# Scores of the late units in 64-column products, a remainder formed by TensorE, and a new order of work

## The chip, the cores and the metric

The kernel runs on one core of a Trainium2 chip. Its time is the device time of one execution in microseconds; several executions are timed and the median is given. The engines named below are TensorE (PE in the rows, PEld its weight loads), VectorE (DVE), ScalarE (ACT), GpSimd (POOL) and SyncE (SP), which issues DMAs.

## What is computed

A gated linear attention with complex gates gives a matrix x of 3072 rows and 384 columns, and a two-layer network with a Gelu is applied to it. Cut to what matters (B = 4, H = 8, S = 768, D = 48, 2048 hidden columns):

```python
scale = np.minimum(mag, 0.999) / (mag + 1e-06)     # mag = |a|
a_re_n, a_im_n = a_re * scale, a_im * scale
for t in range(S):
    ar, ai = a_re_n[:, :, t, :, None], a_im_n[:, :, t, :, None]
    new_re = ar * S_re - ai * S_im
    new_im = ar * S_im + ai * S_re
    S_re, S_im = new_re + k_t[..., None] * v_t[..., None, :], new_im
    y[:, :, t] = einsum('bhd,bhde->bhe', q[:, :, t], S_re)
x = y.transpose(0, 2, 1, 3).reshape(B * S, H * D)
out = gelu(x @ w_in) @ w_out
```

## The kernel before

The scan over time is done in chunks. Within a chunk of 128 (or 64) times the gates are multiplied into queries and keys, the products of keys and queries (the scores) are masked to the causal triangle, and the outputs are scores times values plus queries times the state that the chunk begins with; the state is then brought forward with the products of keys and values. A state has a real and an imaginary part, so the rows over which queries and keys are summed are 96 (2 × 48).

The kernel has four kinds of work. *Lanes* (four groups) run the scan of the gates, on VectorE for the most part (tiles `a`, `bt`, `tt`, `tab`). *Weights* are 32 pieces of w_in and w_out (`wh`, `raw`, `square`), each split into a rounded part and a remainder in F32R (`wi_hi`, `wi_lo`, `wo_hi`, `wo_lo`); TensorE forms the remainder as identity times the piece minus the rounded part (`ident_r`, `minus`). *Units* are 24 pieces of 128 rows of x. The first eight, the early ones, take two chunks of 64 times each, and TensorE turns their keys and queries; units 8 to 23, the late ones, take one chunk of 128 and their keys and queries come turned by DMA; units 20 to 23 end a sequence and bring no state forward. *Blocks* are nine groups of two or three units (2, 3, 3, 3, 3, 3, 3, 2, 2), each with 16 steps f over the hidden columns: `first(f)` makes `ph`, nine F32R products of 256 or 384 columns (three column groups of x, each with rounded part times rounded part, rounded times remainder, remainder times rounded); ScalarE applies the Gelu twice (`gh` rounded, `gf` whole), `gl` is their difference, on VectorE or GpSimd; `second(f)` adds the three products per unit into `po`. Units of block j+1 are recorded among the steps of block j.

Nothing of this is issued where it is written. Every instruction is recorded as a step with what it depends on, and a planner (class `Plan`) chooses its engine, where there are two, and the order on every engine, by list scheduling with costs from the tables at L80 to L101: `MORE` and `WL` weigh the kinds of work against each other, `BIAS` the engines, and `LEAVE` is the cost of going back from a narrow group to a full one. What the recording code joins with `P.together()` stays one group on TensorE. All steps are then issued by `issue` at L422 to L429, so nearly all rows of the profile stand on L429 and are told apart by their tiles.

In a late unit, `scores(hh)` at L922 makes the scores of four heads as four products of 128 keys by 128 queries into one bank of PSUM (`att<-qT,kp`), and VectorE multiplies the 128x512 tile by the triangle `causal` into `kp`. `y(hh)` at L960 makes the outputs from them, 64 columns of the array for each head (`vn` holds the values, two heads lie in the two halves), `y_state` adds queries times state (`att<-qT,st`), and `products` the keys times values for the state (`att<-vn,raw`); these three stand in one group. `turn_state` and `add_state` are the small multiplies and additions of the state (`m`, `st`, `gg`).

At the end of a unit (L1013 to L1027) ScalarE copies the outputs rounded to F32R into x (`x`, `xT` from `att`, 64 and 192 columns wide for an early unit, 128 and 384 for a late one), and VectorE subtracts what was rounded from the outputs in PSUM, which gives the remainder; both go to the block.

Of the kernel before, what the change touches and what calls it, by code (L numbers as in the profile page):

```python
# [10 lines left out]
F32 = mybir.dt.float32  # L11
# [5 lines left out]
ALU = mybir.AluOpType  # L17
# [3 lines left out]
B, H, S, D = 4, 8, 768, 48  # L21
D2 = 2 * D
# [8 lines left out]
NP = 2 * NG  # L31
# [48 lines left out]

ROUND, PASS = 0.462e-3, 0.4219e-3

ENTER, LEAVE = dict(narrow=0.09), dict(narrow=0.2, turn=0.075)
STAY = 1.0
COLD, WARM = 3.0, 4.0
TABLES = {AF.Ln: "natural_log_exp_and_others", AF.Exp: "natural_log_exp_and_others", AF.Gelu: "gelu"}
# [4 lines left out]
UPE = 6  # L91
# [3 lines left out]
EARLIER, N_RAW, N_KP = 1, 4, 2  # L95
PASSES = 4
N_A = 4
WL = 4.532

MORE = dict(lanes0=483.83, lanes1=-1595.06, lanes2=-3639.85, lanes3=-3453.18, weights=-1624.01, units=-66.21, blocks=-85.66)  # L100
BIAS = dict(vector=-0.82, scalar=-1.94, gpsimd=0.93, sync=-6.23)  # L101


class Step:
# [335 lines left out]
def lanes_and_chunks(ctx, tc, flags, a_lanes, x_lanes, v_units, w_in, w_out, out):  # L440
# [10 lines left out]
    causal = cst.tile([128, 128], F32, name="causal")  # L451
# [43 lines left out]
    raw_tiles = [cst.tile([128, H * D2 + 128 - D2], w_in.dtype, name=f"raw{i}", tag=f"raw{i}")[:] for i in range(N_RAW)]  # L495
    for x in raw_tiles:
# [254 lines left out]
    m2s = ring("m2", [D2, 2, DM], 1)  # L751
    qTs = ring("qT", [D2, 4, 128], 2)

    kps = ring("kp", [128, 4, 128], N_KP)
# [31 lines left out]
    def unit(u):  # L786
# [30 lines left out]
        for _, g, m, t0, size, b in chunks:  # L817
# [22 lines left out]
        def turn_state(i, b):  # L840

            sb = st[b]
            tj = next(m2s)[:, 0].rearrange("p (h e) -> p h e", h=H)
            P.sync.dma_start(out=tj[0:D], in_=sb[D:D2])
            P.sync.dma_start(out=tj[D:D2], in_=sb[0:D])
            gg = gain[i - 1][:, :, b * H:(b + 1) * H]
            for x, c in ((sb, 0), (tj, 1)):
                P.either([("vector", "tensor_tensor", (), dict(out=x, in0=x, in1=vap(gg[:, c], [[1, H], [0, D]]), op=ALU.mult))],
                         [("scalar", "mul", (x[:, h, :], x[:, h, :], gg[:, c, h:h + 1]), {}) for h in range(H)])
            P.both("tensor_tensor", out=sb, in0=sb, in1=tj, op=ALU.add)  # L850

        def turn_by_pe(i, b):

            sb = st[b]
            m2 = next(m2s)
            P.vector.tensor_tensor(out=m2.rearrange("p c (h e) -> p c h e", h=H), in0=vap(sb, [[0, 2], [D, H], [1, D]]),
                                   in1=vap(gain[i - 1][:, :, b * H:(b + 1) * H], [[BH, 2], [1, H], [0, D]]), op=ALU.mult)
            whole = bank()[:, 0:DM]
            p = whole[0:D2]
            with P.together():  # L860
                P.tensor.matmul(out=whole, lhsT=ident[0:D2, :], rhs=m2[:, 0], start=True, stop=False)
                P.tensor.matmul(out=whole, lhsT=other_half[:], rhs=m2[:, 1], start=False, stop=True)
            sf = sb.rearrange("p h e -> p (h e)")
            P.either(("scalar", "copy", (sf, p), {}), ("vector", "tensor_copy", (sf, p), {}))
            return whole
# [53 lines left out]
                if dst is kT:  # L919
                    kp.append(t)  # L920

        def scores(hh):  # L922
            p = next(ps_att)
            with P.together():
                for j in range(4):
                    P.tensor.matmul(out=p[:, j * 128:(j + 1) * 128], lhsT=kT[hh][:, j, :], rhs=qT[hh][:, j, :], start=True, stop=True)
            t = kp[hh]
            P.vector.tensor_tensor(out=t, in0=p.rearrange("p (j l) -> p j l", j=4), in1=vap(causal, [[0, 4], [1, 128]]), op=ALU.mult)
            pm.append(t)

        def scores_by_chunk():

# [24 lines left out]
        def y(hh):  # L960
            with P.together():
                for h in range(hh * 4, hh * 4 + 4):
                    P.tensor.matmul(out=py[h % 2 * 64:h % 2 * 64 + 64, h // 2], lhsT=vn[:, h], rhs=pm[hh][:, h % 4], start=h < 2,
                                    stop=h > 5 and not with_state)

        def y_state(chunk, hh):
# [6 lines left out]
        if early:  # L973
            turned = {}
            for c0, c1 in zip(chunks[::2], chunks[1::2]):
                add_state(c0, None)
                turned[c1] = turn_by_pe(c1[0], c1[5])
            turn(0)
            turn(1)
            scores_by_chunk()  # L980
            for c in chunks:
                y_of(c)
            for c in with_state:
                add_state(c, turned[c])
        else:
            for hh in range(2):
                turn(hh)
                if len(chunks) == 1:
                    scores(hh)
# [6 lines left out]
            for c in chunks:  # L996
                turned = p = None
                if c[0]:
                    turned = (turn_by_pe if u < UPE else turn_state)(c[0], c[5])
                with P.together():  # L1000
                    if len(chunks) == 2:
                        y_of(c)
                    else:
                        y(0)
                        y(1)
                        if c[0]:
                            y_state(c, 0)
                            y_state(c, 1)
                    if c[0] < NP - 1:
                        p = products(c, turned)  # L1010
                if p is not None:
                    add_state(c, turned, p)
# [12 lines left out]
        for at, hi, lo, _ in parts:  # L1025
            P.vector.tensor_tensor(out=lo, in0=at, in1=hi.bitcast(F32), op=ALU.subtract)

        if u >= UB:
            x = next(x67d)
# [323 lines left out]
```

## Time and profile before

| | |
|---|---|
| time before, median of 3 runs | 662.56 us (660.89 to 663.44) |
| profiled execution, span | 659.6 us |
| TensorE busy | 614.1 us, 93%, 5154 rows |
| VectorE busy | 484.1 us, 73%, 1204 |
| ScalarE busy | 434.1 us, 66%, 1107 |
| GpSimd busy | 26.1 us, 4%, 74 |

The span runs from the first to the last instruction of the profiled execution, and the time of a run holds what lies around it too. Busy shares are means over stretches that differ, so the rows give them by stretches. Ends of matmuls are modelled; what a matmul costs is better read from the starts of the rows that follow. A product of plain fp32 operands leaves two rows (`x8` for four products of 128 rows by 128 columns) or four (`x32` for eight products in some shapes), an F32R product one. A row of the timeline joins neighbours with the same tiles.

### The profile page before, as it was taken

To read this page: it belongs to the slowest core of one execution; us is meant where nothing else is said; L and a number is where in the kernel's file an instruction comes from. 1 tells how busy PE (TensorE), PEld (TensorE's weight loads), DVE (VectorE), ACT (ScalarE), POOL (GpSimd) and SP (SyncE) were. 2 spreads that over 40 slices of the span, in tenths; PEclk is the share of its full clock that TensorE was granted. 3 is DMA by queue.
4 is the path that set the end of the run, shared out by engine and by line. 5 is a ranking of instruction groups with operands and counts; after the bars stand their busy time and mean duration, and the time that the engine had idled before them with its cause. 6 is when DMAs were issued, how large, how long until landed. Compare 5 with 4: busy or idle time off the path is not lost.

```text
span 659.6 us, 13997 instructions
## 1 busy us (share of the span) xinstructions
PE 614.1 (93%) x5154; PEld 563.8 (85%) x5154; DVE 484.1 (73%) x1204; ACT 434.1 (66%) x1107; POOL 26.1 (4%) x74
## 2 busy tenths in 40 slices
PE   4655499999999999999999999999999999999995
PEld 2322277988789999999999999999999999999995
DVE  6999999999999999999989999656334424232211
ACT  8976699999998979787476997535442422232332
POOL 1000100002000000120000000020000000000000
PEclk9787699999999999999999999999999999999999
DMA  9366876668266456687889966487444132110000
GB/s 322 119 158 161 256 225 212 185 196 258 71 197 173 116 135 177 163 173 158 198 198 219 230 157 166 116 167 169 104 88 88 50 64 46 34 51 15 25 1 27
DMA packets 210442, 93.51 MB, mean 142 GB/s; under 512 B 167744, under 2 KB 202688, under 8 KB 210368
## 3 DMA queue, kind: packets, MB, share of 16 engines
q1 hardware_dynamic: 210368, 92.57, 54.6%
q8 instruction: 41, 0.67, 0.4%
q14 instruction: 33, 0.27, 0.1%
HBM read 63.11 MB, written 25.69 MB: 135 GB/s over the span
## 4 chain that ended last, share of the span: by engine, by line
PE 70%; ACT 9%; DVE 9%; issue 2%; DMA 1%; SPq 0%; DVEq 0%; ACTq 0%
PE po L429 27%; PE ph L429 26%; PE att L429 17%; DVE a L429 2%; ACT a L429 1%; DVE tt L429 1%; ACT tab L429 1%; ACT L429 1%; ACT L427 1%; DVE xt L429 1%; ACT gh L429 1%; DVE bt L429 1%; ACT gf L429 1%; DMA raw<-in_w_pieces_dram 1%; ACT square L429 1%
## 5 line engine op out<-in xcount | busy, mean ns | idle before, releaser
L429 PE MATMUL ph<-xT,wi_hi 128*128 128x384 f32 (+1 forms) x864 | 209.2, 324 | 0.0
L429 DVE TENSOR_TENSOR gl<-gf,gh 128x384 fp32r<-128x384 f32 (+1 forms) x144 | 73.7, 512 | 126.4 <-ACT gf L429 126.0
L429 ACT ACTIVATE gh<-ph 128x384 fp32r<-128x384 f32 (+1 forms) x144 | 65.8, 457 | 149.6 <-PE ph L429 149.2
L429 PEld LDWEIGHTS ph<-xT,wi_hi 128*128 128x128 f32 x864 | 154.3, 188 | 2.2 <-ACT gf L429 0.2
L429 PE MATMUL ph<-xT,wi_lo 128*128 128x384 f32 (+1 forms) x432 | 137.3, 318 | 0.0
L429 PE MATMUL po<-wo_hi,gh 128*128 128x384 f32 x384 | 132.5, 345 | 0.9 <-ACT gh L429 0.7
L429 PE MATMUL po<-wo_lo,gh 128*128 128x384 f32 x384 | 129.7, 338 | 0.0
L429 PE MATMUL po<-wo_hi,gl 128*128 128x384 f32 x384 | 92.5, 342 | 0.0
L429 PEld LDWEIGHTS ph<-xT,wi_lo 128*128 128x128 f32 x432 | 81.3, 188 | 0.1
L429 PEld LDWEIGHTS po<-wo_hi,gh 128*128 128x128 f32 x384 | 72.1, 188 | 3.0 <-ACT gh L429 2.0
L429 PEld LDWEIGHTS po<-wo_lo,gh 128*128 128x128 f32 x384 | 72.5, 189 | 0.0
L429 DVE TENSOR_TENSOR tt<-bt,a 128x192 f32<-128x192 f32 x192 | 67.3, 350 | 0.5
L429 PEld LDWEIGHTS po<-wo_hi,gl 128*128 128x128 f32 x384 | 65.9, 188 | 1.6 <-DVE gl L429 0.7
L429 ACT ACTIVATE gf<-ph 128x384 f32<-128x384 f32 (+1 forms) x144 | 65.4, 454 | 2.5 <-DVE gl L429 2.5
L429 DVE TENSOR_TENSOR bt<-tt 128x96 f32<-128x96 f32 x192 | 48.1, 250 | 0.5
L429 PEld LDWEIGHTS att<-qT,kp 96*64 96x64 f32 (+1 forms) x512 | 39.4, 165 | 2.4 <-issue 1.5
L429 PE MATMUL att<-qT,kp 96*64 96x64 f32 (+1 forms) x512 | 41.0, 250 | 0.0
L429 DVE TENSOR_TENSOR kp<-att,causal 128x512 f32<-128x512 f32 x40 | 27.5, 687 | 9.5 <-PE att L429 9.4
L429 ACT ACTIVATE a<-tab 128x384 f32<-128x384 f32 (+1 forms) x48 | 25.6, 534 | 9.3 <-DVE tab L429 9.2
L429 PE MATMUL po<-wh,ident_r 128*128 128x384 f32 x48 | 22.0, 541 | 9.4 <-DVE wh L429 9.3
L429 PE MATMUL att<-tab,ident_r 128*128 128x384 f32 (+1 forms) x20 | 14.8, 896 | 13.6 <-ACT tab L429 13.6
L429 ACT ACT_TABLE_LOAD x21 | 26.9, 1283 | 0.3
(154 smaller groups left out, 992.9 us busy)
## 6 DMA issues: line engine op xcount, KB each, us to landing
kqn<-kq SPq DMA_DIRECT2D x96, 128.0 KB, 3.2
xt<-in_x_lanes_dram SPq DMA_DIRECT2D x24, 384.0 KB, 4.4
kq<-xt SPq DMA_DIRECT2D x48, 192.0 KB, 3.5
a<-in_a_lanes_dram SPq DMA_DIRECT2D x20, 384.0 KB, 3.4
raw<-in_w_pieces_dram SPq DMA_DIRECT2D x16, 384.0 KB, 4.1
raw<-in_moe_w_out_dram SPq DMA_DIRECT2D x16, 384.0 KB, 4.3
vn<-in_v_units_dram SPq DMA_DIRECT2D x24, 256.0 KB, 3.7
kqn<-kq SPq DMA_DIRECT2D x8, 768.0 KB, 5.7
```

What stands on the lines that cost most here:

```text
L427: self.nc.scalar.preload_act_table_set(table)
L429: getattr(getattr(self.nc, engine), name)(*args, **kw)
```

## The change

The scores of a late unit are made as two products per head: keys 0 to 63 by all 128 queries, and keys 64 to 127 by queries 64 to 127. The quarter that the mask would clear isn't computed. In odd heads the two halves of the keys lie swapped in PSUM (`p0 = l0 ^ h % 2 * 64`), so a second mask is made for them (`causals`), and their values are copied with halves swapped into `v_odd`, in room that the second half of the tile `m2` gives. The mask's multiply stays on VectorE in the same size. The scores of all eight heads stand in one group with the products for the state, where there are any; the masks, `turn_state`, and then a group of outputs and state follow.

In an early unit the remainder of x is formed on TensorE: the rounded part times `minus` is added to the outputs in PSUM, and the result is copied out by ScalarE or VectorE. Late units keep the subtraction on VectorE. Two raw tiles lose 32 columns of padding. The planner's `LEAVE`, `WL`, `MORE` and `BIAS` have new values, so the order is another one everywhere.

```diff
-ENTER, LEAVE = dict(narrow=0.09), dict(narrow=0.2, turn=0.075)
+ENTER, LEAVE = dict(narrow=0.09), dict(narrow=0.09, turn=0.075)
...
-WL = 4.532
-MORE = dict(lanes0=483.83, lanes1=-1595.06, lanes2=-3639.85, ...
+WL = 0.649
+MORE = dict(lanes0=1387.58, lanes1=868.97, lanes2=111.91, ...
...
+    for p0 in (0, 64):
+        nc.gpsimd.tensor_copy(causals[p0:p0 + 64, 1, 64 - p0:128 - p0], causal[p0:p0 + 64, p0:p0 + 64])
+        nc.gpsimd.memset(causals[p0:p0 + 64, 1, p0:p0 + 64], p0 / 64)
...
+    m2_whole = next(ring("m2", [128, 2, DM], 1))
+    m2 = m2_whole[0:D2]
+    v_odd = m2_whole[:, 1, 0:H // 2 * D + 64 - D]
...
+        if by_dve:
+            for p0 in (0, 64):
+                swapped = v_odd[64 - p0:128 - p0, 0:H // 2 * D].rearrange("p (h d) -> p h d", d=D), vn[p0:p0 + 64, 1::2, 0:D]
+                P.either(("scalar", "copy", swapped, {}), ("vector", "tensor_copy", swapped, {}))
...
-        def scores(hh):
-            p = next(ps_att)
-            with P.together():
-                for j in range(4):
-                    P.tensor.matmul(out=p[:, j * 128:(j + 1) * 128], lhsT=kT[hh][:, j, :], rhs=qT[hh][:, j, :], start=True, stop=True)
+        def scores():
+            ps_hh = [next(ps_att) for _ in range(2)]
+            for h in range(H):
+                hh, j = divmod(h, 4)
+                p = ps_hh[hh][:, j * 128:(j + 1) * 128]
+                for l0 in (0, 64):
+                    p0 = l0 ^ h % 2 * 64
+                    P.tensor.matmul(out=p[p0:p0 + 64, l0:128], lhsT=kT[hh][:, j, l0:l0 + 64], rhs=qT[hh][:, j, l0:128], start=True, stop=True)
...
+                    v = v_odd[:, h // 2 * D:h // 2 * D + 64] if h % 2 else vn[:, h]
+                    P.tensor.matmul(out=py[h % 2 * 64:h % 2 * 64 + 64, h // 2], lhsT=v, rhs=pm[hh][:, h % 4], start=h < 2,
...
+                with P.together():
+                    ps_hh = scores()
+                    if c[0] < NP - 1:
+                        p = products(c, None)
+                for hh in range(2):
+                    mask(hh, ps_hh[hh])
+                turn_state(c[0], c[5])
...
                 with P.together():
+                    y(0)
+                    y(1)
+                    y_state(c, 0)
+                    y_state(c, 1)
...
+        if by_dve:
+            for at, hi, lo, _ in parts:
+                P.vector.tensor_tensor(out=lo, in0=at, in1=hi.bitcast(F32), op=ALU.subtract)
+        else:
+            with P.together():
+                for at, hi, _, _ in parts:
+                    P.tensor.matmul(out=at, lhsT=minus[:], rhs=hi, start=False, stop=True, skip_group_check=True)
+            for at, _, lo, _ in parts:
+                P.either(("scalar", "copy", (lo, at), {}), ("vector", "tensor_copy", (lo, at), {}))
```

By counts: narrow groups on TensorE (products of at most 64 columns of the array between F32R products) go from 42 to 58; ScalarE's multiplies of 96x48 from 144 to 40, with 13 more multiplies of 96x384 on VectorE; ScalarE gets all 32 swapping copies and 30 of the 32 copies of the remainder; GpSimd gets some 13 operations of the lanes and 5 of the 144 `gl`; ScalarE's table loads go from 45 to 43, and DMAs stay at 624.

The order at three places follows. On TensorE, a late unit amid a block before (scores `att<-qT,kp`, outputs `att<-kp,vn`, state `att<-qT,st`, products `att<-vn,raw`):

```order
L429 MATMUL att_110<-qT_149,kp_151 128x128 x4
L429 MATMUL att_108<-qT_150,kp_152 128x128 x4
L429 MATMUL ph_111<-xT_153,wi_hi 128x384 x2
L429 MATMUL ph_111<-xT_153,wi_lo 128x384
L429 MATMUL po_113<-wo_hi,gl_164 128x384
L429 MATMUL po_114<-wo_hi,gl_164 128x384
L429 MATMUL po_115<-wo_hi,gl_164 128x384
L429 MATMUL att_109<-kp_151,vn_146 64x128 x4
L429 MATMUL att_109<-kp_152,vn_146 64x128 x4
L429 MATMUL att_109<-qT_149,st_158 48x128 x4
L429 MATMUL att_109<-qT_150,st_158 48x128 x4
L429 MATMUL att_110<-vn_146,raw_116 64x48 x16
```

The two score groups stand alone, six F32R products lie between them and one narrow group of outputs, state and products. And a late unit after (`m` is `v_odd`), up to its outputs:

```order
L429 MATMUL att_114<-qT_153,kp_155 64x128
L429 MATMUL att_114<-qT_153,kp_155 64x64
L429 MATMUL att_112<-vn_148,raw_120 64x48 x16
L429 MATMUL ph_115<-xT_156,wi_hi 128x384 x2
L429 MATMUL ph_115<-xT_156,wi_lo 128x384
L429 MATMUL po_117<-wo_hi,gl_167 128x384
L429 MATMUL po_118<-wo_hi,gl_167 128x384
L429 MATMUL po_119<-wo_hi,gl_167 128x384
```

The products now follow the scores at once, in their group; behind two more rows of F32R products come the outputs, which are a group of their own with the state.

On TensorE ahead of the first block's first product, before (last row; `wh` a weight piece, `att<-qT,kp` scores of an early unit):

```order
L429 MATMUL po_115<-wh_125,ident_r 128x384
L429 MATMUL po_115<-wo_hi,minus 128x384
L429 MATMUL po_115<-wo_lo,minus 128x384
L429 MATMUL att_109<-kp_151,vn_146 64x64 x8
L429 MATMUL att_110<-vn_146,kqn_144 64x48 x16
L429 MATMUL ph_111<-xT_153,wi_hi 128x256 x2
```

and after, with the products of `minus` that form the remainder of x:

```order
L429 MATMUL po_117<-x_158,minus 128x64
L429 MATMUL po_117<-xT_156,minus 128x192
L429 MATMUL po_118<-x_158,minus 128x64
L429 MATMUL po_118<-xT_156,minus 128x192
L429 MATMUL po_119<-wh_127,ident_r 128x384
L429 MATMUL po_119<-wo_hi,minus 128x384
L429 MATMUL po_119<-wo_lo,minus 128x384
L429 MATMUL att_113<-kp_154,vn_148 64x64 x8
L429 MATMUL att_114<-vn_148,kqn_146 64x48 x16
L429 MATMUL po_119<-wh_126,ident_r 128x384
L429 MATMUL po_119<-wi_hi,minus 128x384
```

The products of `minus` are new there, and more weight pieces and more of the next unit come ahead too: the first block's first product (`ph<-xT,wi_hi`) was row 109 of TensorE and is row 130.

On ScalarE ahead of the first Gelu, before:

```order
L429 ACTIVATE tab_133<-tab_133 128x384
L429 ACTIVATE xT_154,flags<-att_109 128x3x64
L429 ACTIVATE x_155,flags<-att_109 128x64
L429 ACTIVATE a_130<-a_130 128x432
L429 ACTIVATE square_126,flags<-raw_118 128x384
L429 COPY st_160<-att_108 96x384
L429 ACT_TABLE_LOAD
L429 ACTIVATE gh_162<-ph_111 128x256
```

and after, where `CAST x` and `CAST xT` are the copies of the remainder:

```order
L429 COPY st_163<-att_112 96x384
L429 CAST wo_lo<-po_119 128x384
L429 CAST xT_157<-att_113 128x3x64
L429 CAST x_158<-att_113 128x64
L429 ACTIVATE a_129,flags<-tab_135 128x384
L429 CAST x_158<-att_114 128x64
L429 CAST xT_157<-att_114 128x3x64
L429 ACT_TABLE_LOAD
L429 ACTIVATE gh_165<-ph_115 128x256
```

Four copies of the remainder and a weight's copy stand there now; the first Gelu (`gh`) was row 191 of ScalarE and is row 211.

## Rows read from the trace of the kernel before

**Rows 1.** Stretches: length, busy us (count) of PE, PEld, DVE, ACT, POOL, PEclk, DMA, GB/s.

```profile
0.00:83.00 83.00, 45.40 (x94) 23.66 (x95) 73.81 (x202) 64.24 (x158) 6.38 (x33) 0.80 0.68 205
83.00:190.00 107.00, 106.43 (x1291) 88.83 (x1291) 103.60 (x280) 105.26 (x279) 6.33 (x14) 1.00 0.63 187
190.00:652.00 462.00, 461.56 (x3768) 451.04 (x3766) 306.56 (x723) 263.76 (x669) 13.38 (x27) 1.00 0.51 121
```

**Rows 2.** Chain of waits from 83 to 190 us, its head line.

```profile
by line: PE att L429 18.6%; PE ph L429 13.1%; PE po L429 12.5%; DVE tt L429 4.3%; ACT square L429 4.1%; ACT a L429 3.9%; ACT L427 3.6%; ACT L429 3.6%; DVE a L429 3.4%; issue 3.1%; DVE wh L429 3.0%; ACT tab L429 2.6%; ACT gh L429 2.4%; DVE b
```

**Rows 3.** TensorE's timeline at four full scores: start, length, operation, rows.

```profile
385.12 0.51 PE L429 MATMUL ph<-xT,wi_hi 128*128 128x384 f32 x2
385.47 0.34 PE L429 MATMUL ph<-xT,wi_lo 128*128 128x384 f32 x1
385.65 1.06 PE L429 MATMUL att<-qT,kp 96*128 96x128 f32 x8
...
386.72 0.34 PE L429 MATMUL po<-wo_lo,gh 128*128 128x384 f32 x1
```

**Rows 4.** TensorE's timeline at a late unit's outputs, state and products.

```profile
392.15 0.34 PE L429 MATMUL ph<-xT,wi_lo 128*128 128x384 f32 x1
...
393.35 1.05 PE L429 MATMUL att<-qT,st 96*48 96x128 f32 x16
394.22 1.09 PE L429 MATMUL att<-vn,raw 128*64 128x48 f32 x32
395.24 0.62 PE L429 MATMUL ph<-xT,wi_hi 128*128 128x384 f32 x2
395.70 0.34 PE L429 MATMUL ph<-xT,wi_lo 128*128 128x384 f32 x1
```

**Rows 5.** TensorE's timeline at an early unit's sixteen narrow scores.

```profile
208.11 0.34 PE L429 MATMUL po<-wo_lo,gh 128*128 128x384 f32 x1
208.38 1.15 PE L429 MATMUL att<-qT,kp 96*64 96x64 f32 x32
...
209.74 0.34 PE L429 MATMUL po<-wo_lo,gh 128*128 128x384 f32 x1
```

**Rows 6.** TensorE's timeline at outputs and state of a unit without products.

```profile
524.22 0.34 PE L429 MATMUL po<-wo_lo,gh 128*128 128x384 f32 x1
524.49 1.09 PE L429 MATMUL att<-kp,vn 128*64 128x128 f32 x16
...
526.39 0.79 PE L429 MATMUL po<-wo_hi,gl 128*128 128x384 f32 x3
527.02 0.52 PE L429 MATMUL ph<-xT,wi_hi 128*128 128x384 f32 x2
```

**Rows 7.** Groups by line and form: count, busy us, mean ns, idle before and releaser.

```profile
L429 DVE TENSOR_TENSOR xT<-att,xT 128x192 fp32r<-128x192 f32 x12 | 4.2, 349 | 0.0
L429 DVE TENSOR_TENSOR x<-att,x 128x64 fp32r<-128x64 f32 x12 | 2.6, 217 | 0.2 <-ACT x L429 0.2
L429 ACT ACTIVATE xT<-att 128x192 fp32r<-128x192 f32 x12 | 4.0, 333 | 0.0
L429 ACT ACTIVATE x<-att 128x64 fp32r<-128x64 f32 x12 | 2.8, 232 | 0.6 <-DMA kq<-xt 0.6
L429 ACT ACTIVATE st<-st,gg 96x48 f32<-96x48 f32 x80 | 19.1, 325 | 0.0
L429 DVE TENSOR_TENSOR gl<-gf,gh 128x384 fp32r<-128x384 f32 x96 | 53.2, 555 | 75.0 <-ACT gf L429 74.5
```

**Rows 8.** TensorE's timeline at eight F32R products of 128 columns.

```profile
120.40 0.69 PE L429 MATMUL att<-ident_r,kqn 128*96 128x128 f32 x8
120.93 0.47 PE L429 MATMUL ph<-xT,wi_hi 128*128 128x256 f32 x2
```

**Rows 9.** ScalarE's timeline at the first Gelu.

```profile
116.29 0.38 ACT L429 ACTIVATE gh<-ph 128x256 fp32r<-128x256 f32 x1
```

**Rows 10.** TensorE's timeline at the first product that reads it.

```profile
117.58 0.34 PE L429 MATMUL po<-wo_hi,gh 128*128 128x384 f32 x1
```

More of the change, by code (lines that the diff above doesn't have):

```diff
@@ L97 @@
 N_A = 4
-WL = 4.532
-MORE = dict(lanes0=483.83, lanes1=-1595.06, lanes2=-3639.85, lanes3=-3453.18, weights=-1624.01, units=-66.21, blocks=-85.66)
-BIAS = dict(vector=-0.82, scalar=-1.94, gpsimd=0.93, sync=-6.23)
+WL = 0.649
+MORE = dict(lanes0=1387.58, lanes1=868.97, lanes2=111.91, lanes3=-49.23, weights=814.32, units=2140.78, blocks=1344.97)
+BIAS = dict(vector=1.05, scalar=0.18, gpsimd=1.12, sync=-6.23)
 class Step:
@@ L449, in ring @@
         return itertools.cycle([pool.tile(shape, dtype, name=f"{name}{i}", tag=f"{name}{i}")[:] for i in range(n)])
-    causal = cst.tile([128, 128], F32, name="causal")
+    causals = cst.tile([128, 2, 128], F32, name="causals")
+    causal = causals[:, 0]
     make_identity(nc, causal)
@@ L494, in lanes_and_chunks @@
     ps_h = itertools.cycle(ph)
-    raw_tiles = [cst.tile([128, H * D2 + 128 - D2], w_in.dtype, name=f"raw{i}", tag=f"raw{i}")[:] for i in range(N_RAW)]
-    for x in raw_tiles:
+    raw_tiles = [cst.tile([128, H * D2 + (128 - D2) * (i < 2)], w_in.dtype, name=f"raw{i}", tag=f"raw{i}")[:] for i in range(N_RAW)]
+    for x in raw_tiles[:2]:
         nc.gpsimd.memset(x.bitcast(F32)[:, H * D2:], 0.0)
@@ L750, in lanes_and_chunks @@
     vns = ring("vn", [128, H, 64], 2)
-    m2s = ring("m2", [D2, 2, DM], 1)
+    m2_whole = next(ring("m2", [128, 2, DM], 1))
+    m2 = m2_whole[0:D2]
+    v_odd = m2_whole[:, 1, 0:H // 2 * D + 64 - D]
+    nc.gpsimd.memset(v_odd, 0.0)
     qTs = ring("qT", [D2, 4, 128], 2)
@@ L842, in turn_state @@
             sb = st[b]
-            tj = next(m2s)[:, 0].rearrange("p (h e) -> p h e", h=H)
+            tj = m2[:, 0].rearrange("p (h e) -> p h e", h=H)
             P.sync.dma_start(out=tj[0:D], in_=sb[D:D2])
@@ L854, in turn_by_pe @@
             sb = st[b]
-            m2 = next(m2s)
             P.vector.tensor_tensor(out=m2.rearrange("p c (h e) -> p c h e", h=H), in0=vap(sb, [[0, 2], [D, H], [1, D]]),
@@ L920, in turn, with mask @@
                     kp.append(t)
-        def scores(hh):
-            p = next(ps_att)
-            with P.together():
-                for j in range(4):
-                    P.tensor.matmul(out=p[:, j * 128:(j + 1) * 128], lhsT=kT[hh][:, j, :], rhs=qT[hh][:, j, :], start=True, stop=True)
+        def scores():
[6 more added lines that the diff above has]
+                    P.tensor.matmul(out=p[p0:p0 + 64, l0:128], lhsT=kT[hh][:, j, l0:l0 + 64], rhs=qT[hh][:, j, l0:128], start=True, stop=True)
+            return ps_hh
+        def mask(hh, p):
             t = kp[hh]
-            P.vector.tensor_tensor(out=t, in0=p.rearrange("p (j l) -> p j l", j=4), in1=vap(causal, [[0, 4], [1, 128]]), op=ALU.mult)
+            P.vector.tensor_tensor(out=t.rearrange("p (j s) l -> p j s l", s=2), in0=p.rearrange("p (j s l) -> p j s l", j=2, s=2),
+                                   in1=vap(causals, [[0, 2], [128, 2], [1, 128]]), op=ALU.mult)
             pm.append(t)
@@ L962, in y @@
                 for h in range(hh * 4, hh * 4 + 4):
-                    P.tensor.matmul(out=py[h % 2 * 64:h % 2 * 64 + 64, h // 2], lhsT=vn[:, h], rhs=pm[hh][:, h % 4], start=h < 2,
+                    v = v_odd[:, h // 2 * D:h // 2 * D + 64] if h % 2 else vn[:, h]
+                    P.tensor.matmul(out=py[h % 2 * 64:h % 2 * 64 + 64, h // 2], lhsT=v, rhs=pm[hh][:, h % 4], start=h < 2,
                                     stop=h > 5 and not with_state)
@@ L987, in unit @@
                 turn(hh)
-                if len(chunks) == 1:
-                    scores(hh)
             if len(chunks) == 2:
                 scores_by_chunk()
-            else:
+                for c in chunks:
+                    turned = p = None
+                    if c[0]:
+                        turned = (turn_by_pe if u < UPE else turn_state)(c[0], c[5])
+                    with P.together():
+                        y_of(c)
+                        if c[0] < NP - 1:
+                            p = products(c, turned)
+                    if p is not None:
+                        add_state(c, turned, p)
+            else:
+                c = chunks[0]
+                p = None
+                with P.together():
+                    ps_hh = scores()
+                    if c[0] < NP - 1:
+                        p = products(c, None)
+                for hh in range(2):
+                    mask(hh, ps_hh[hh])
+                turn_state(c[0], c[5])
                 held.append(bank())
@@ L995, in unit @@
                 pys.append((py, 0, C))
[L996 to L999, printed above, removed]
                 with P.together():
[L1001 to L1010, printed above, removed]
+                    y(0)
+                    y(1)
+                    y_state(c, 0)
+                    y_state(c, 1)
                 if p is not None:
-                    add_state(c, turned, p)
+                    add_state(c, None, p)
         j = next(j for j in range(len(BLOCKS)) if u < first_unit[j + 1])
@@ L1024, in unit @@
             P.scalar.activation(hi, at, AF.Copy, accum_out=flags[:, f:f + 1])
-        for at, hi, lo, _ in parts:
-            P.vector.tensor_tensor(out=lo, in0=at, in1=hi.bitcast(F32), op=ALU.subtract)
+        if by_dve:
+            for at, hi, lo, _ in parts:
+                P.vector.tensor_tensor(out=lo, in0=at, in1=hi.bitcast(F32), op=ALU.subtract)
+        else:
+            with P.together():
+                for at, hi, _, _ in parts:
+                    P.tensor.matmul(out=at, lhsT=minus[:], rhs=hi, start=False, stop=True, skip_group_check=True)
+            for at, _, lo, _ in parts:
+                P.either(("scalar", "copy", (lo, at), {}), ("vector", "tensor_copy", (lo, at), {}))
         if u >= UB:
```

## The prediction

> **What bounds the kernel now.** I read the busy time by stretches first [rows 1]. In the first 83 us TensorE works 45.40 us and stands for the other 37.6, while VectorE is busy for 73.81 and ScalarE for 64.24: the start is bound by the scan of the gates and by the making of the first inputs. From 83 to 190 us TensorE is busy for 106.43 of 107.00 us, VectorE for 103.60, ScalarE for 105.26: three full engines. From 190 to 652 only TensorE is full (461.56 of 462.00; VectorE 306.56, ScalarE 263.76). The span is 659.6 us, so some 7.6 us of tail follow. Second, the chain of waits for the middle stretch [rows 2]: the three TensorE lines hold 18.6 + 13.1 + 12.5 = 44% of it, and pieces of VectorE and ScalarE most of the rest. So the stretch is the one place where a change off TensorE might count; behind 190 us only what TensorE does counts, and it is told in durations of TensorE alone.
>
> I read TensorE's prices from starts, since the ends are modelled. The granted clock is 1.00 (2.4 GHz) in both later stretches [rows 1], so one set of prices serves. Two F32R products of 384 columns start .35 apart (385.12 to 385.47), so one costs .175 [rows 3].
>
> **Scores of the late units** (8 to 23, sixteen of them). Before, four heads come as one full group: from 385.47 to 386.72 lie 1.25 us, which hold two F32R products (.35) and the four scores: .90, or .225 a head and 1.80 a unit [rows 3]. After, each head has a product of 128 columns and one of 64, each on half of the array. Nearest row for 128: the eight products of queries with the state, 393.35 to 394.22, .87 or .109 each [rows 4]. For 64: the early units' scores. 208.11 to 209.74 is 1.63; less two F32R products and less the .356 of a narrow group (below), 16 products cost .92, .058 each [rows 5]. So a head costs .167 and a unit 1.34, a gain of .46, and sixteen give 7.4 us.
>
> This price is one end. In those rows neighbouring products alternate between the two halves of the array's columns. In the new order keys 0 to 63 of an even head go to the lower half, keys 64 to 127 to the upper, and in an odd head the other way round; so every second pair of neighbours is on one half. No row of before shows what that costs. Nothing excludes the dearer end: with no overlap at all a head is 2 × .167 = .334, 1.34 us a unit more than I take, 21 us over the sum. The likely dearer value is the full product's price, .225 [rows 3], which gives back all of the 7.4. I take .167, since one pair in two still alternates as in the rows it comes from [rows 4, 5].
>
> **One more narrow group per late unit.** Products of 64 columns of the array stand in groups between F32R products of 128. What entering and leaving such a group costs: in a unit that has no products at its end, 524.22 to 527.02 is 2.80 us, which hold four F32R products (.70) and 16 products at .109 (1.74): .356 stays over [rows 6]. Full scores show no such rest, since they are full-width themselves [rows 3]. Before, a late unit had one narrow group (outputs, state, products in one: 392.15 to 395.70, 3.55 us, less .525 is 3.03, and less 2.10 for outputs and state leaves .92 for 16 products, .058 each [rows 4]). After, scores are narrow too, with the products in their group, and outputs and state form the second. That is 16 groups more, 16 × .356 = 5.7 us. Below, entry alone is .095 (524.22 to the first narrow product at 524.49, less .175 [rows 6]), 1.5 us for sixteen; above, the .356 is a whole group's and I see no reason for more. I take the whole.
>
> The Trainium skill, TensorEngine Tiling (Array Packing), Key Properties, says that a change of the tiling mode drains TensorE, and so speaks against a second narrow group. The trace agrees, with .356 us for a group [rows 6]; if the drains cost nothing, the sum would be 5.7 us lower, if they were each as they are read there it stays.
>
> **Remainder of x in the early units.** 32 subtractions leave VectorE, 16 of 128x192 at .349 and 16 of 128x64 at .217: 9.1 us [rows 7]. Instead TensorE adds 32 F32R products. Nearest rows: eight of 128 columns in .53 (120.40 to 120.93), .066 each, which I take for 64 columns, and .09 for 192, between this and .175 for 384 [rows 3, 8]: 16 × .156 = 2.5 us. For no less than 0 and no more than .175 each it would be 0 to 5.6. The products read x's rounded part, so they wait for ScalarE; all but the first unit's lie behind other work of TensorE. The copies that follow go nearly all to ScalarE, 15 + 15 of 32, at .232 and .333 by its copies of these shapes [rows 7]: up to 8.5 us more there. That ends in the middle stretch, where ScalarE is as full as the others [rows 1], and so it isn't free.
>
> **Start and first block.** Ahead of the first block's first product TensorE now has two more weight pieces (six F32R products), two turns of state (.35), 32 small products, eight of the new subtractions and two group changes: 1.05 + .35 + 32 × .058 + 4 × .156 + .71 = 4.6 us. ScalarE comes to the first Gelu with 20 more instructions; at .33 each (its shapes in [rows 7]) that is 6.6 us. Before, the first Gelu began at 116.29 and ended by 116.67, and the product that reads it came at 117.58 [rows 9, 10]: .9 us of slack. 6.6 − 4.6 − .9 = 1.1, and I take 1 us that TensorE now waits. By the mean of all ScalarE instructions in the stretch (105.26 / 279 = .38 [rows 1]) it is 2 and more if the small rows wait for their inputs; from below, the 9.1 us that VectorE loses may take away the wait and up to 3 us of what is there now. What TensorE did early it doesn't do later, so only the wait counts.
>
> **What is hidden.** Behind 190 us ScalarE loses 104 small multiplies (.325 each, 34 us) and gains 32 copies that swap the halves of v for odd heads (some 10 us at .33); VectorE gains 13 multiplies of 96x384 (7 us at the .555 that the Gelu's remainder of 384 columns takes) [rows 7]. Both have over 150 us to spare there [rows 1], so I cost this at nothing; without that cover the gain would be ScalarE's 24 us. Some 13 operations of the gates' scan and 5 subtractions of the Gelu's remainder move to GpSimd, whose instructions average .50 us there [rows 1] against VectorE's .555 [rows 7]; its longer ones aren't told apart, so from 0 to 5 × 1 us; zero, since a block's remainder products stand last in their step. Two masks of 512 columns, 4/3 × .555 = .74 each [rows 7], now have to fit between the scores and the outputs, where TensorE has 16 products (.92) and mostly 8 to 12 F32R products (1.4 to 2.1): 2.3 us or more against 1.5. No DMA is added. Four small GpSimd setups lie in the first 83 us, where TensorE stands anyway.
>
> **Sum.** The profiled execution's span, 659.6, is 3.0 below the median of the runs, 662.56; I add 3.0 to what comes out. 659.6 − 7.4 + 5.7 + 2.5 + 1 = 661.4, with the 3.0 some **664.5 us**: +0.3%, within the 0.5% (3.3 us: below 659.2 or above 665.9) that a measurement of this kernel can tell from no change.
>
> **Rivals.** A, slower: neighbours on the same half don't overlap and a head keeps costing .225. For it: every second pair; against: the rest alternate as in the rows. It gives 664.5 + 7.4 = 671.9, and decides from about .19 a head on (16 × 8 × .023 = 2.9). The Trainium skill, TensorE: Matmul & The Clock Gate, part 2, says that weights may be loaded ahead but matmuls stay in program order; that would make a waiting product of the same half hold the other half's product too. No row here shows it.
>
> B, faster: the middle stretch is really held by VectorE. For it: TensorE's lines are only 44% of the chain [rows 2], and 9.1 us leave VectorE, most of them there. Against it: TensorE is busy 106.43 of 107.00 [rows 1]. If 6 of the 9.1 come off the stretch and ScalarE doesn't lag, 664.5 − 1 − 6 = 657.5.
>
> C, slower: ScalarE's 8.5 us of copies and its 20 earlier instructions hold the first block by 5 us instead of 1: 668.5. For it: ScalarE is 98% busy [rows 1]; against: the slack of .9 and less work for it later.
>
> That the narrow scores aren't run as narrow is excluded by the order itself; that they gain and the groups cost nothing is the end of 1.5 instead of 5.7, which is 660.3, still within.
>
> **Chances.** Forecast .38 (counted as no change), A .22, B .28, C .12. So faster .28, same .38, slower .34. The range takes in B, the forecast, C and A: 655 to 673; beyond it lie the 21 us without overlap, and more than 9 us of gain.
>
> **What would show it.** In the profile after: eight heads' scores and the products in one group, which should take 1.34 + .92 + .36 = 2.6 us beside F32R neighbours (3.1 by A); outputs and state 2.1; TensorE idle in the first 83 us near 37.6 and in 83 to 190 near .6, with more of it by C and with the first blocks' products earlier by B. The forecast is wrong if TensorE is idle for over 2 us anywhere behind 83 us, if the span up to the last early unit's end changes by more than 3 us, or if the start changes with the new order.

## The result and the profile after

The changed kernel takes 666.82 us (median of 6 runs, 665.61 to 669.66), the kernel before beside it 662.38. The ratio is 1.0066, with a 95% interval of 1.0041 to 1.0092: slower by 4.4 us. The forecast was 664.5 us in a range of 655 to 673, with "no change" as the likeliest case; the range holds the time, and the measured case is the one of slower by over 0.5%, if barely.

The profiled execution of the result has a span of 668.0 us and was one of the slower ones; the same kernel, run twice more, left spans of 665.2 and 665.0 (medians 667.59 and 667.68). The first of these is used for stretches. Its busy time by stretches, to be laid beside [rows 1] (columns as there):

```profile
0.00:83.00 83.00, 46.36 (x145) 25.64 (x145) 75.23 (x208) 67.63 (x166) 6.88 (x36) 0.79 0.71 215
83.00:190.00 107.00, 103.50 (x1255) 86.46 (x1254) 101.07 (x263) 102.35 (x293) 13.40 (x16) 1.00 0.61 182
190.00:652.00 462.00, 460.77 (x4023) 442.32 (x4022) 306.71 (x699) 255.23 (x607) 31.59 (x42) 1.00 0.52 121
```

Before, TensorE stood .57 us in the middle stretch and .44 behind it; now it stands 3.50 and 1.23. VectorE, which lost 32 subtractions, isn't full there any more (101.07 of 107, before 103.60), and neither is ScalarE (102.35, before 105.26). The waits of TensorE in the middle have several releasers, none of them large (waited for, us, times, longest):

```profile
PE po L429 <- ACT gh L429: 0.9, 2, 0.4
PE att L429 <- DVE m L429: 0.8, 1, 0.8
PE att L429 <- ACT x L429: 0.7, 1, 0.7
PE att L429 <- ACT kp L429: 0.5, 1, 0.5
PE att L429 <- DMA kqn<-kq: 0.3, 1, 0.3
```

Those that name ScalarE come to 2.1 us, where before had .5, and the one that names VectorE to .8, where before had none.

A late unit's scores and products in the first trace of the changed kernel, TensorE's timeline, with the F32R products around them (compare [rows 3, 4]):

```profile
349.26 0.34 PE L429 MATMUL po<-wo_lo,gh 128*128 128x384 f32 x1
349.53 1.56 PE L429 MATMUL att<-qT,kp 96*64 96x128 f32 x32
350.92 1.09 PE L429 MATMUL att<-vn,raw 128*64 128x48 f32 x32
351.94 0.44 PE L429 MATMUL po<-wo_hi,gh 128*128 128x384 f32 x1
352.22 0.34 PE L429 MATMUL po<-wo_lo,gh 128*128 128x384 f32 x1
```

From 349.26 to 352.22 lie 2.96 us; less two F32R products, 2.61. The prediction said 2.6, or 3.1 if neighbours on one half of the array don't overlap. They do: 2.61 less the .92 of the products and the .356 of a group leaves 1.33 for eight heads, .167 a head. The outputs' group takes 2.10 as in [rows 6] (same trace, a unit 8 us on):

```profile
357.49 0.34 PE L429 MATMUL ph<-xT,wi_lo 128*128 128x384 f32 x1
...
358.68 1.04 PE L429 MATMUL att<-qT,st 96*48 96x128 f32 x16
359.66 0.44 PE L429 MATMUL po<-wo_hi,gh 128*128 128x384 f32 x1
359.94 0.34 PE L429 MATMUL po<-wo_lo,gh 128*128 128x384 f32 x1
```

(357.49 to 359.94 is 2.45, less .35.) So a late unit costs 2.61 + 2.10 = 4.71 us of TensorE, and cost 1.79 + 3.02 = 4.81: a tenth of a us less, 1.6 us for sixteen, which is the -7.4 + 5.7 of the sum. The four units without products come out alike: their scores cost 1.79 before, alone between full products, and cost 1.69 as a narrow group of their own.

The remainder in an early unit, TensorE's timeline in the first trace, and below it two products of the first block for comparison:

```profile
104.92 0.30 PE L429 MATMUL po<-x,minus 128*128 128x64 f32 x1
105.05 0.33 PE L429 MATMUL po<-xT,minus 128*128 128x192 f32 x1
105.23 0.22 PE L429 MATMUL po<-x,minus 128*128 128x64 f32 x1
105.28 0.34 PE L429 MATMUL po<-xT,minus 128*128 128x192 f32 x1
105.45 0.83 PE L429 MATMUL po<-wh,ident_r 128*128 128x384 f32 x2
...
116.06 0.28 PE L429 MATMUL ph<-xT,wi_lo 128*128 128x256 f32 x1
116.18 0.40 PE L429 MATMUL ph<-xT,wi_hi 128*128 128x256 f32 x2
```

From 104.92 to 105.45 it is .53 for this unit, which comes right behind a narrow group. The last five units take .42 to .43 each, and all 32 products, from their starts to the starts of what follows, take 4.05 us in each of the three traces, not 2.5. The products of 192 columns hold TensorE for .17 to .18, longer than a product of 256 columns (.12, from 116.06 to 116.18).

Last, the end. SyncE's timeline has the last output DMA of before at 653.63 of 659.6 us:

```profile
653.63 0.33 SPq L429 DMA_DIRECT2D out_dram<-wh  x1
```

and that of the changed kernel (the last of its three traces) at 656.37 of 665.0:

```profile
656.37 0.38 SPq L429 DMA_DIRECT2D out_dram<-wh  x1
```

So 2.7 us of that trace's 5.4 come behind the last output DMA: 8.6 us of tail against 6.0. In the other two traces of the changed kernel it is 2.1 and 2.2. The prediction had no term for the tail.

### The profile page after: what moved, and what is told of

Same layout as the page of the kernel before. It is cut to its first block, busy times and chain, and to the rows that moved or that the text cites. A ratio compares the mean times of both kernels' runs of the same rounds, so it can differ in the third digit from the quotient of the medians.

```text
span 668.0 us, 14515 instructions
## 1 busy us (share of the span) xinstructions
PE 619.1 (93%) x5442; PEld 559.9 (84%) x5442; DVE 484.6 (73%) x1171; ACT 428.0 (64%) x1069; POOL 52.6 (8%) x94
## 4 chain that ended last, share of the span: by engine, by line
PE 68%; ACT 10%; DVE 7%; DMA 4%; issue 2%; SPq 0%; DVEq 0%; ACTq 0%
PE po L429 27%; PE ph L429 26%; PE att L429 14%; DMA kqn<-kq 2%; ACT a L429 2%; ACT square L429 2%; DVE a L429 1%; DMA xT<-x 1%; ACT L429 1%; DVE tt L429 1%; ACT gh L429 1%; DVE kp L429 1%; ACT L427 1%; DVE bt L429 1%; DMA raw<-in_w_pieces_dram 1%
## 5 line engine op out<-in xcount | busy, mean ns | idle before, releaser
L429 DVE TENSOR_TENSOR gl<-gf,gh 128x384 fp32r<-128x384 f32 (+1 forms) x139 | 71.3, 513 | 137.3 <-ACT gf L429 135.5
L429 DVE TENSOR_TENSOR tt<-bt,a 128x192 f32<-128x192 f32 x192 | 69.0, 359 | 1.0
L429 PEld LDWEIGHTS att<-qT,kp 96*64 96x64 f32 x768 | 30.8, 137 | 7.1 <-issue 4.1
L429 PE MATMUL att<-qT,kp 96*64 96x64 f32 (+1 forms) x768 | 34.4, 242 | 0.3
L429 PEld LDWEIGHTS att<-kp,vn 64*64 64x64 f32 (+1 forms) x320 | 20.0, 135 | 7.4 <-issue 3.3
L429 PE MATMUL att<-kp,vn 64*64 64x64 f32 (+1 forms) x320 | 25.7, 246 | 0.4 <-DVE kp L429 0.4
```

Of the source, the lines that this page charges most:

```text
L429: getattr(getattr(self.nc, engine), name)(*args, **kw)
```

## The experiments

Where it is said that the order is kept, the planner plans for the steps of the kernel named, and only when an instruction is issued is another put in its place, so that all others stand as they stood. The times are medians; before is 662.4 to 663.3 in each group of runs.

**The changed kernel once more.** No edit.

> The changed kernel once more, unaltered, as the base for the runs beside it. Expected 666.8 us against 662.4 of before, a ratio near 1.007, and a second trace: waits of TensorE between 83 and 190 us that belong to the order come again (4 to 5 us in the first trace of after against 0.5 of before), those of one execution don't.

667.59 us, ratio 1.0067 (1.0047 to 1.0088). The middle's waits came again (3.5 us of TensorE standing, above); the wait of 1.7 us for `kqn` that the first trace had in the middle is .3 here and belongs to that execution.

**Full scores, order and groups kept.**

```diff
-    two products per head: keys 0-63 x 128 queries, keys 64-127 x queries 64-127   # in short
+    matmul(out=ps_hh[h // 4][:, h % 4 * 128:(h % 4 + 1) * 128], lhsT=kT[h // 4][:, h % 4, :], rhs=qT[h // 4][:, h % 4, :])
...
-    y: lhsT = v_odd for odd heads   # in short
+    y: lhsT = vn[:, h]
```

> The changed kernel with its order and its groups kept, and only the late units' scores made again as one full product of 128 keys by 128 queries per head (triangle mask and values as before the change; the swapping copies are still issued). If a head in narrow products costs 0.167 us against 0.225, as read from the starts, 16 x 8 x 0.058 = 7.4 us come back: 674 us. If neighbours on the same half don't overlap beyond what a full product costs, nothing: 667 us. The number of narrow groups is the same, since the products of the state stay behind the scores.

672.05 us, ratio 1.0129 (1.0101 to 1.0158): 4.5 us more than the changed kernel by the medians, 7.0 more by the spans (672.2 against 665.2). In its trace the same group:

```profile
349.61 0.34 PE L430 MATMUL po<-wo_lo,gh 128*128 128x384 f32 x1
349.79 1.95 PE L430 MATMUL att<-qT,kp 96*128 96x128 f32 x16
351.67 1.14 PE L430 MATMUL att<-vn,raw 128*64 128x48 f32 x32
352.74 0.44 PE L430 MATMUL po<-wo_hi,gh 128*128 128x384 f32 x1
353.01 0.34 PE L430 MATMUL po<-wo_lo,gh 128*128 128x384 f32 x1
```

From 349.61 to 353.01 are 3.40 against 2.96, .44 a unit, and so it is in the twelve units that have products. The expectation overlooked the four units without: there full scores stand alone and open no narrow group, and cost 1.79 against 1.69, .10 a unit. 12 × .44 + 4 × .10 is 5.7 us, not 7.4, and the medians' 4.5 fits that better; the spans are of single executions. The price of a head is as forecast; rival A, on which the slower side mostly rested, falls.

**Products one F32R step behind the scores**: twelve narrow groups more, no work more, order kept.

> The changed kernel with its order kept, except that in the twelve late units with a state product these products stand one F32R step behind the scores instead of in their group: twelve narrow groups more and no work more. If a group costs 0.356 us, 12 x 0.356 = 4.3 us more than the changed kernel: 672 us. If only entry cost something (0.095), 1.1 us: 668.7 us.

671.62 us, ratio 1.0136 (1.0113 to 1.0159): 4.0 us more than the changed kernel by the medians, 4.6 by the ratios, 4.3 expected. In its trace:

```profile
348.73 0.34 PE L430 MATMUL po<-wo_lo,gh 128*128 128x384 f32 x1
349.00 1.56 PE L430 MATMUL att<-qT,kp 96*64 96x128 f32 x32
...
350.77 0.34 PE L430 MATMUL po<-wo_lo,gh 128*128 128x384 f32 x1
351.04 1.14 PE L433 MATMUL att<-vn,raw 128*64 128x48 f32 x32
...
352.56 0.34 PE L430 MATMUL ph<-xT,wi_lo 128*128 128x384 f32 x1
```

The scores take 2.04 less two F32R products, 1.69, and the products 1.79 less three, 1.27. Together that is 2.96 against the 2.61 of the joined group, so a group costs .35, which was read from [rows 6] as .356. The gain of the narrow scores (.46 a unit) and the price of the extra group nearly cancel, and both are real.

**Narrow scores in the order of before**, in the twelve late units whose halves stand together:

```diff
-    matmul(out=p[:, j * 128:(j + 1) * 128], lhsT=kT[hh][:, j, :], rhs=qT[hh][:, j, :])
+    for l0 in (0, 64):   # p0 = l0 ^ j % 2 * 64
+        matmul(out=p[p0:p0 + 64, j * 128 + l0:(j + 1) * 128], lhsT=kT[hh][:, j, l0:l0 + 64], rhs=qT[hh][:, j, l0:128])
...
```

> The kernel before with its order kept; of the change only the scores in two products per head (with the swapped values), in the twelve late units where both halves of the heads stand together on TensorE; the products of the state stay with the outputs. Twelve narrow groups more at 0.356 and twelve times 0.46 less: -1.2 us, 661.3 us, which this measurement can hardly tell from no change. Were a head 0.225 in narrow products too, it would be 4.3 us more: 667 us; were the groups free, 5.5 less: 657 us.

662.51 us, ratio .9985 (.9955 to 1.0014): no change that could be told, as the sum wants it. In its trace each of the twelve score groups takes 1.69 us instead of 1.79, which is the -1.2 us of the expectation.

**The remainder back on VectorE, order kept.**

```diff
-    matmul(out=at, lhsT=minus, rhs=hi, start=False)      # 32 products
-    scalar.copy(lo, at)                                  # 30 on ScalarE, 2 on VectorE
+    vector.tensor_tensor(out=lo, in0=at, in1=hi, op=subtract)
```

> The changed kernel with its order kept, and only the remainder of x in the early units back on VectorE: the 32 products with minus are not issued, and each copy is a subtraction on VectorE at the copy's place in the order. If TensorE's sum holds, 2.5 to 4 us go (the trace of after has 4.05 us between the starts of these 32 products and what follows them), perhaps 1 more since x comes one engine sooner: 662 to 664 us. If VectorE's relief was worth something in the middle stretch, it is gone with it: 667 to 671 us.

668.11 us, ratio 1.0073 (1.0038 to 1.0109): no gain that could be told, though the interval leaves room for some 2 us. TensorE has 4 us less to do, and waits more instead. Its middle stretch, and the waits there:

```profile
83.00:190.00 107.00, 101.23 (x1233) 84.32 (x1233) 103.84 (x283) 100.39 (x274) 13.66 (x16) 1.00 0.60 180
```
```profile
PE att L430 <- DVE m L430: 1.6, 1, 1.6
PE att L430 <- DVE kp L430: 1.2, 1, 1.2
PE po L430 <- DVE gl L430: 1.1, 2, 0.7
```

TensorE stands 5.77 us there instead of 3.50, and the waits that name VectorE come to 3.9 us instead of .8. So the relief of VectorE was worth something, about 2.3 us in this stretch, and it paid for a part of the 4.05: what rival B said, at some 40% of its size.

**The copies of the remainder on VectorE, order kept**, all 32 in place of 2.

> The changed kernel with its order kept, the products with minus kept, and all copies of the remainder issued to VectorE instead of 30 of 32 to ScalarE. TensorE's work stays. If ScalarE's load of 8.5 us were what makes TensorE wait in the middle, 1 to 3 us go: 665 us. If VectorE is what TensorE waits for, as in the run with the subtraction back on VectorE (2.4 us more waits), it rises to 669 to 670 us. If neither counts, 667.6 us.

669.66 us, ratio 1.0134 (1.0088 to 1.0180), as the second expectation has it. The middle, and the waits there that name VectorE:

```profile
83.00:190.00 107.00, 102.65 (x1232) 84.93 (x1232) 101.56 (x277) 98.71 (x266) 13.45 (x16) 0.98 0.60 179
```
```profile
PE att L430 <- DVE m L430: 1.6, 1, 1.6
PE po L430 <- DVE gl L430: 0.7, 1, 0.7
PE att L430 <- DVE kp L430: 0.7, 1, 0.7
```

ScalarE is relieved (98.71 against 102.35) and TensorE stands 4.35 us, not less. The waits that name ScalarE fall from 2.1 to .9 us, and those that name VectorE rise from .8 to 3.0. So ScalarE's copies hold the middle a little, and on VectorE they hold it more. In this trace TensorE also had the half clock (1.2 GHz, .50) from 111.4 to 114.8, hence the .98, so its time isn't the copies' alone. Rival C had 5 us of waiting; in the changed kernel the waits that name ScalarE are 1.6 us more than in before, so its size falls, its cause only in part.

**The remainder on TensorE in the order of before**: in the place of each subtraction a product and ScalarE's copy.

> The kernel before with its order kept; of the change only the early units' remainder: in the place of each of VectorE's 32 subtractions stand a product with minus on TensorE and a copy on ScalarE. TensorE gets 3.7 to 4 us (as between the starts in the trace of after), VectorE loses 9.1 us, ScalarE gets up to 8.5. If TensorE's sum decides, 666 us. If VectorE's relief in the middle stretch pays, as it did when the subtraction went back (2.4 us), 663 to 664 us. If ScalarE holds the middle, over 667 us.

676.59 us, ratio 1.0188 (1.0139 to 1.0237), on the side of the third expectation and far beyond it. The middle and the waits:

```profile
83.00:190.00 107.00, 102.97 (x1177) 84.17 (x1178) 94.59 (x246) 101.59 (x286) 5.88 (x14) 0.97 0.61 180
```
```profile
PE att L430 <- ACT a L430: 1.9, 1, 1.9
PE po L430 <- ACT x L430: 1.1, 2, 0.8
PE att L430 <- ACT xT L430: 0.4, 1, 0.4
```

VectorE is busy for 9 us less there (94.59 against 103.60) and TensorE's waits name ScalarE now: the product reads ScalarE's rounded copy, and the kept order has nothing between them. That is 1.7 us; the 1.9 us for `a` aren't the remainder's. More of the loss lies elsewhere. TensorE from 80 to 90 us, before and in this run:

```profile
80.00:90.00 10.00, 9.37 (x95) 6.60 (x95) 9.73 (x26) 8.89 (x23) 0.00 (x0) 0.80 0.86 280
```
```profile
80.00:90.00 10.00, 8.15 (x42) 4.78 (x42) 8.73 (x26) 7.17 (x17) 0.00 (x0) 0.52 1.04 335
```

It had the lower granted clock for longer there (.52 against .80 in the mean) and got through 42 products instead of 95. At the scores of an early unit (95.04 us, in before 90.67) it is 4.4 us behind, and the first product that the run adds comes only at 101.80. Of the 17.2 us between the two spans these 4.4 are the start's and 2.2 the tail's, so the run is no price of the remainder in the old order; what the rest is stays open.

**The constants exchanged.** The changed code planned with the old constants, the old code with the new ones, and the late scores alone with the old ones.

> All of the changed code, with the planner's four constants (LEAVE, WL, MORE, BIAS) of before, so that the order is planned anew with those. By TensorE's sum the code alone is worth -1.6 us for the scores and +2.5 to +4 for the remainder, so 663 to 665 us if the new constants' order is what costs the rest; about 667 us or more if the order isn't to blame, or if the old constants don't suit the new steps.

666.43 us, ratio 1.0044 (1.0024 to 1.0063), no more than with the new constants (1.0067, 1.0047 to 1.0088). The middle has fewer waits than with these, 1.84 us:

```profile
83.00:190.00 107.00, 105.16 (x1279) 89.12 (x1276) 102.19 (x271) 104.65 (x289) 5.96 (x14) 1.00 0.63 188
```

> The kernel before with nothing but the planner's new constants (LEAVE, WL, MORE, BIAS). If the new order itself costs the waits of TensorE between 83 and 200 us, it shows without any of the new code: 664 to 666 us, with some 2 to 3 us more waits there than before's. If the waits come from the new code, 662 to 663 us.

685.73 us, ratio 1.0341 (1.0309 to 1.0374), 23 us slower with no code changed. TensorE's stretches:

```profile
83.00:190.00 107.00, 99.55 (x1166) 82.31 (x1166) 99.54 (x269) 98.26 (x259) 10.79 (x15) 0.98 0.58 170
190.00:652.00 462.00, 452.89 (x3747) 437.05 (x3746) 315.00 (x715) 258.80 (x629) 36.56 (x45) 1.00 0.52 125
```

It stands 7.5 us in the middle and 9.1 behind 190 us, where before it stood .57 and .44.

> Of the change only the late units' scores (with their groups and swapped values); the remainder of x is VectorE's subtraction again, and the planner has its constants of before. By TensorE's sum 16 x (0.46 - 0.36) = 1.6 us go: 661 us, or 0.5 to 1 us less than the sum if the new plan brings waits. If the late units' new groups cost waits of their own (both masks between two groups), 664 to 666 us, and the trace has TensorE wait for VectorE's masks behind 290 us.

685.23 us, ratio 1.0343 (1.0318 to 1.0368), where 661 was expected: a miss of 24 us. It is the plan rather than the scores, since the scores in the kept order cost nothing. The waits behind 83 us (up to 640):

```profile
PE po L429 <- ACT gh L429: 7.7, 7, 4.9
PE ph L429 <- ACT gf L429: 3.1, 2, 2.7
PE att L429 <- DVE kp L429: 1.4, 2, 1.2
```

Mostly it is the Gelu that comes late, and the masks only a little. So a plan can be worth 23 us by itself: constants that suit one set of steps (the old ones suit all of the changed code too) can be bad for another. The two kernels compared here are each planned with constants of their own.

**Ten more instructions on SyncE.** In the trace, with all its semaphore and register instructions, SyncE has 745 records in before and 737 in the changed kernel. Behind the last output DMA come a branch and then eight instructions on semaphores in a row. In before these follow each other in .07 to .1 us; in the changed kernel there are 1.6 to 1.8 us between the seventh and the eighth, and with 743 records (the old constants) 2.1 us between the first and the second: six records fewer, six further on. So the stop stands at a fixed number of SyncE's instructions. Eleven of the fourteen traces here have such a stop, of 1.2 to 2.3 us: ten right before SyncE's 724th record and one before the 725th. The instruction that stands there changes with the count, and the last DMA on its semaphore landed over 30 us earlier in every one of them, so SyncE doesn't wait for a DMA there.

```diff
+    if k == len(steps) * 19 // 20:
+        for i in range(10):
+            nc.sync.dma_start(out=scratch[i:i + 1], in_=v_units[0][i:i + 1, 0, 0:16])
```

> The changed kernel with nothing changed but ten DMAs of at most 64 bytes (DRAM to DRAM, into a scratch nobody reads) on SyncE at 95% of the order, where SyncE has nothing to do. In the trace of before 5.95 us lie between SyncE's last output DMA and the end of the span, in those of after 8.0 to 8.2, and in the latter SyncE stands still 1.6 us between two of its last semaphore instructions. If that is a fetch of SyncE's code, whose place depends only on how many instructions SyncE has had (745 in before's trace, 737 in after's), ten more instructions move it ahead, into an earlier wait: tail near 6 us, and the time 2 us less, 664.5 to 665.5 us. If the tail comes from the late work itself, it stays 8 us and the time 667 us.

> The changed kernel unaltered, as the base for the run beside it on the same chip: 667 us, ratio near 1.007 to before, tail near 8.1 us in the trace.

665.44 us against 667.68 of the changed kernel beside it; ratios 1.0032 (1.0009 to 1.0056) and 1.0064 (1.0043 to 1.0086). In its trace (span 663.6) the last output DMA stands at 657.01,

```profile
657.01 0.37 SPq L433 DMA_DIRECT2D out_dram<-wh  x1
```

so the tail is 6.6 us instead of 8.6, and the stop between the semaphores is gone; the last output DMA itself comes no earlier than beside it (656.37). About half of the loss is this. In all other traces here the tail follows the same count: 5.9 us with 745 records (the narrow scores in the order of before), 7.6 to 8.8 with 731 to 743.

That the stop is a fetch of SyncE's code isn't shown. Behind 650 us the two queues of instruction code carry six and two packets in the changed kernel and five and two with the ten DMAs more, but five and two with the old constants as well, where SyncE stands 2.1 us. Nor is the stop all of the tail: SyncE also stands behind the branch, 2.7 us in before, 3.0 to 3.5 in the changed kernel and 1.9 with the old constants, and no run tells why.

No run here beats the kernel before: the nearest is the narrow scores in its order, the same within .3%.

## Why the prediction came out as it did

- **Scores and groups: right.** -7.4 and +5.7 were read from rows of other products, and the trace after has them at .46 and .36 a unit; the runs with full scores (.44 a unit where there are products) and with twelve more groups (.35 each) bear out both. Rival A, at .22, was the risk of a price that no row showed; swapping the halves in odd heads costs TensorE nothing.
- **Remainder of x: the mechanism right, the term too small.** 2.5 us were taken from products of 128 columns; it is 4.05. The bounds (0 to 5.6) held it. The relief of VectorE was costed at nothing in the sum and left to rival B; the run with the subtraction back on VectorE has 2.3 us of it in the middle, and no difference in time that could be told. That 4.05 less 2.3 comes near the 2.5 is luck.
- **Start and first block: 1 us was too small, and the place was wrong.** The first block's first product came at 115.75, 114.32 and 113.51 in the three traces, against 110.32 in before. That is 3.2 to 5.4 us later; the 4.6 us that the sum gave to the work put ahead would cover most of it. But the waits are spread over 83 to 190 us with several releasers (3.5 us standing against .57), VectorE and DMAs among them. Two of the prediction's own signs that it would be wrong came true: over 2 us of standing behind 83 us, and the last early unit's copies, which begin 3.1 to 6.7 us earlier than the subtractions of before did (249.03). With the old constants the same code stands 1.84 us in the middle, so the new order makes somewhat over half of the new standing; which moves do it stays open.
- **Hidden work: right.** Behind 190 us ScalarE and VectorE stay far from full, and TensorE stands .8 us more than before. No wait of TensorE there or in the middle names GpSimd.
- **What the sum left out: the tail.** It starts from the span of before, 659.6, and so took the tail in that span as fixed. The tail grew by 2.1 to 2.7 us. Most of that is the stop of SyncE, whose place moves with the number of its instructions; the rest is a longer wait behind the branch. Without the stop the changed kernel stands at 1.0032, 2.1 us over before, and the sum had said 1.9. That the two are so near is partly luck, since the remainder and the standing were both priced too low.

The parts of the work close only roughly. Up to the last output DMA the second trace takes 3.4 us more than before (657.02 against 653.63), and the third 2.7, where the sum had 1.8. The parts read above are -1.6, +4.05, and 2.9 and .8 of standing, less 1.0 that TensorE does more in the first 83 us. They make 5.2 against the 3.4 of that trace. TensorE's busy time is modelled at its ends, and its records tell standing from a slow product badly; the 1.8 us between stay open. So half of the loss has a cause shown by a run, the tail; the other half is the remainder and the new order, and how much each takes isn't shown.

## What to carry to other kernels

A quarter of masked work can be left out by narrower products, but most of the gain goes if that opens one more narrow group between full ones: here .46 us of gain met .36 of entry and exit. An operation moved from a full engine to another that is full as well need not gain anything: here 4.05 us of products bought 2.3 us less standing in the middle. Price the relief too, by the waits that name the relieved engine. An order made by a planner belongs to the exact steps it was made for: keep the order when testing a part, and don't read a part's worth from a replanned kernel. For a difference of 0.5%, read the end of the program too: here about half of it stood behind the last output DMA.

## What the runs showed of the hardware

The end of the program is not free. SyncE's last instructions stood 1.2 to 2.3 us at one place in eleven of fourteen traces, nearly always right before its 724th record, and ten small DMAs earlier on the same engine took 2.2 us from the kernel's time (667.68 to 665.44). A group of products of 64 columns of the array between F32R products of 128 cost .35 us for entry and exit. Products of which every second pair lies on the same half of the array cost no more than alternating ones (.167 us a head either way); none here lie on one half throughout. An F32R product of 192 columns added to outputs in PSUM held TensorE .17 to .18 us, more than one of 256 columns elsewhere (.12); why wasn't tried.
